# Chunked attention and two feed-forward layers: raw tiles of the next pair loaded from GpSimd's queue

## The chip, the cores and the metric

The kernel runs on one core of a Trainium2 chip. The metric is the device time of one execution in microseconds: 1698.02 us, the median of 3 runs (1697.63 to 1699.63). The core's engines run instruction streams of their own, each strictly in order: TensorE (PE; its weight loads are PEld), VectorE (DVE), ScalarE (ACT), GpSimd (POOL) and SyncE (SP). An engine waits for another through semaphores. A DMA is started by an instruction in the stream of one engine, called that engine's queue here, and is carried out by the core's 16 DMA engines; its completion raises a semaphore.

## The reference

```
attention, per batch (8), head (8) and chunk of 64 rows (576 = 9 chunks), head_dim 64:
    attn = softmax(q_c @ k_c^T / 8);   out_c = attn @ v_c
x = out as [4608 tokens, 512]
first layer:   h = x @ w_in;   g = s * relu(h)^2 + b;          y = g @ w_out     (512 -> 2048 -> 512)
second layer:  h = y @ w2_in;  g = h * sigmoid(1.702 * h);   out = g @ w2_out    (512 -> 2048 -> 512)
```

The weights of both layers come as float64 and are decoded to float32 on the chip. The change touches the second layer alone, and of it the way in which y is read back.

## The kernel before

The 4608 tokens are nine blocks of 512. Each float32 operand of a product is split into a high and a low part, and a product is three matmuls (low x high, high x high, high x low). The first layer runs block by block (L403 into h, L446 into acc) and stores its result y of each block to DRAM, features on partitions, as tiles y0 to y8 (y_140 to y_147 in listings are blocks 1 to 8). The second layer of block 0 runs the same way.

The other eight blocks of the second layer are computed in four pairs by `Halves`: features and tokens are both cut in two, and seven products M1 to M7 of sums of quarters stand for the eight products of the plain scheme. Each pair has two phases:

- First phase (L542): eight groups i of products, each of which leaves four quarters of h in PSUM banks named x, d and b. `keep` copies partial results out (L550, tile kept). `quarter` adds them (L561), takes the sigmoid (L563, tile r) and multiplies (L564) into g, held in tiles wo. Quarter "21" reads the bank x itself (L563 and L564 with the input x). Its bank is one of the tags acc0 to acc3; the last group, i = 7, has acc3.
- Second phase (L637): the seven products of g with the sums of w2_out. An operand is split by ACT (L614) and DVE (L615) into gh and gl, or op. M1's results need the banks acc2 and acc3, one for each half z of the output features.

The sums of the weights lie in DRAM (wi_sums, wo_sums) and are loaded by SP into tiles wi as these come free: L524 for the first phase, L597 for the second, 28 loads of 512 KB a pair. A tile wi comes free when PE has read it, so each of these loads waits for PE in SP's stream.

The operand x of the next pair is prepared while the present pair is in its second phase. `load_x(k)` (L481) loads four raw quarters of y into tiles xr of 128 x 512 float32 (256 KB each), for k = 0 and then for k = 1: b11, b12, b22 and b21, in that order. `operands_x(k)` then splits and subtracts them (L496 on ACT, L497 and L467 on DVE, tiles xh, xl and others). That is 8 loads a pair and 32 in all. The tiles xr come from the pool tpool (tag tmp, 10 buffers in rotation), which also holds kept, r and the output tiles ost; a load into one of them waits until the earlier user of that buffer has been read.

What sets the order: the program hands out its steps with due times (`plan`, `plan_first`, `plan_second`; the call `at`), sorted, and a scheduler then puts them into one fixed stream per engine. load_x(0) of the next pair falls due one unit after the second phase of the present pair begins, `operands_x(0)` three units later.

Of the kernel before, what the change touches and what calls it, by code (L numbers as in the profile page):

```python
# [59 lines left out]
def chunk_attention_two_ffn(ctx, tc, q, k, v, w1_in, w1_out, s, b, w2_in, w2_out, out):  # L60
# [6 lines left out]
    nc = tc.nc  # L67
# [37 lines left out]
    y_dram = [dpool.tile([P, KD, n], F32, name=f"y{j}") for j, n in enumerate(sizes)]  # L105
# [7 lines left out]
    def tmp(name, dtype=F32):  # L113
        return tpool.tile([P, NB_MAX], dtype, tag="tmp", name=name)
# [349 lines left out]
    HF, HK = KF // 2, KD // 2  # L464
# [4 lines left out]
    class Halves:  # L469
# [7 lines left out]
        def load_x(self, k):  # L477
            self.raw = getattr(self, "raw", {})
            for (a, c) in ((0, 0), (0, 1), (1, 1), (1, 0)):
                t = tmp("xr")  # L480
                nc.sync.dma_start(out=t, in_=y_dram[self.j + c][:, k + a * HK, :])  # L481
                self.raw[k, a, c] = t

        def x_place(self, n):
# [230 lines left out]
    for n, (i, kind) in enumerate((i, kind) for i in range(KF // 2) for kind in ("wi", "wo")):  # L715
        t = NS + 3 + 13.5 * n
# [45 lines left out]
```

## Time and profile before

| what | value |
|---|---|
| median of the runs | 1698.02 us |
| the profiled execution: time, and its span | 1698.26 us, 1696.5 us |
| mean granted TensorE clock | 0.984 |
| PE busy | 1603.6 us, 95% of the span |
| DVE / ACT / POOL busy | 1198.1 / 722.8 / 345.6 us |
| DMA moved | 263.79 MB, mean 155 GB/s |
| loads xr, all on SP | 32 of 256 KB, median 5.4 us from issue to landing |

How to read it: PE is the engine that is nearly always busy, so that time is lost where PE waits. The granted clock of 1.00 is TensorE's upper level, 2.4 GHz; its lower level is 1.2 GHz. POOL has no work after 973 us of the span. The four pairs run from about 1045 us to the end.

### The profile page before, as it was taken

To read this page: it belongs to the slowest core of one execution; us is meant where nothing else is said; L and a number is where in the kernel's file an instruction comes from. 1 tells how busy PE (TensorE), PEld (TensorE's weight loads), DVE (VectorE), ACT (ScalarE), POOL (GpSimd) and SP (SyncE) were. 2 spreads that over 40 slices of the span, in tenths; PEclk is the share of its full clock that TensorE was granted. 3 is DMA by queue.
4 is the path that set the end of the run, shared out by engine and by line. 5 is a ranking of instruction groups with operands and counts; after the bars stand their busy time and mean duration, and the time that the engine had idled before them with its cause. 6 is when DMAs were issued, how large, how long until landed. Compare 5 with 4: busy or idle time off the path is not lost.

```text
span 1696.5 us, 24510 instructions
## 1 busy us (share of the span) xinstructions
PE 1603.6 (95%) x8864; PEld 1317.1 (78%) x8864; DVE 1198.1 (71%) x1844; ACT 722.8 (43%) x1194; POOL 345.6 (20%) x310
## 2 busy tenths in 40 slices
PE   4767999999999999999999999989998999899998
PEld 3545788888878888888888888878886888688876
DVE  6999976868877686877833343579557946884685
ACT  3555533334333333433334433456345525553552
POOL 2677522222222223232315400000000000000000
PEclk9988999999999999999999999999999999999999
DMA  8733454655555465555324341667866686677664
GB/s 192 192 94 72 118 131 125 154 130 144 133 145 135 120 156 135 153 135 140 112 88 138 102 134 44 193 209 227 207 193 218 206 221 202 206 209 219 209 199 81
DMA packets 407128, 263.79 MB, mean 155 GB/s; under 512 B 264160, under 2 KB 354272, under 8 KB 407008
## 3 DMA queue, kind: packets, MB, share of 16 engines
q1 hardware_dynamic: 407008, 262.23, 56.4%
q8 instruction: 70, 1.15, 0.3%
q14 instruction: 50, 0.41, 0.1%
HBM read 205.52 MB, written 56.62 MB: 155 GB/s over the span
## 4 chain that ended last, share of the span: by engine, by line
PE 79%; DVE 12%; DMA 3%; SPq 2%; ACT 1%; issue 1%; POOL 0%; DVEq 0%; ACTq 0%; POOLq 0%
PE acc L446 21%; PE h L403 21%; PE x L637 10%; PE x L542 10%; PE d L637 5%; PE d L542 5%; PE b L637 3%; PE b L542 2%; DVE pt L300 2%; PE xT L308 2%; PE sc L274 1%; DVE r L412 1%; DMA xr<-y 1%; DMA wst<-in_moe_w_in 1%; SPq L246 1%
## 5 line engine op out<-in xcount | busy, mean ns | idle before, releaser
L403 PE MATMUL h<-xh,wi 128*128 128x512 f32 x1280 | 401.4, 395 | 9.5 <-ACT r L411 6.7
L446 PE MATMUL acc<-gh,wo 128*128 128x512 f32 x1152 | 359.2, 395 | 19.4 <-ACT gh L416 11.0
L403 PEld LDWEIGHTS h<-xh,wi 128*128 128x128 f32 x1280 | 242.3, 191 | 61.9 <-issue 10.0
L446 PEld LDWEIGHTS acc<-gh,wo 128*128 128x128 f32 x1152 | 216.8, 190 | 66.1 <-issue 9.4
L403 PE MATMUL h<-xl,wi 128*128 128x512 f32 x640 | 251.0, 393 | 0.0
L446 PE MATMUL acc<-gl,wo 128*128 128x512 f32 x576 | 224.4, 392 | 4.1 <-POOL gl L417 4.1
L412 DVE SCALAR_TENSOR_TENSOR r<-r,sb 128x512 f32<-128x512 f32 x144 | 137.2, 954 | 103.0 <-ACT r L411 102.5
L420 DVE SCALAR_TENSOR_TENSOR gl<-r,sb,gh 128x512 fp32r<-128x512 f32 x128 | 125.6, 981 | 70.6 <-ACT gh L419 70.4
L419 ACT ACTIVATE gh<-r,sb 128x512 fp32r<-128x512 f32 x128 | 92.6, 723 | 172.4 <-DVE r L412 171.6
L411 ACT ACTIVATE r<-h 128x512 f32<-128x512 f32 x144 | 85.1, 592 | 143.7 <-PE h L403 138.1
L403 PEld LDWEIGHTS h<-xl,wi 128*128 128x128 f32 x640 | 121.6, 190 | 25.8
L446 PEld LDWEIGHTS acc<-gl,wo 128*128 128x128 f32 x576 | 108.2, 188 | 27.9 <-POOL gl L417 4.9
L300 DVE STREAM_TRANSPOSE pt<-p 32x256 f32<-32x256 f32 x288 | 125.6, 436 | 4.8
L141 POOL TENSOR_TENSOR wm<-wm,wc 128x512 int32<-128x512 int32 x42 | 61.3, 1459 | 262.9 <-ACT gh L419 117.6
L614 ACT ACTIVATE op<-wo 128x512 fp32r<-128x512 f32 x128 | 79.9, 631 | 80.9 <-PE x L637 27.8
L564 DVE TENSOR_TENSOR wo<-wo,r 128x512 f32<-128x512 f32 x96 | 66.0, 691 | 63.4 <-ACT r L563 62.9
L637 PE MATMUL x<-op,wi 128*128 128x512 f32 x432 | 104.9, 390 | 0.0
L542 PE MATMUL x<-xh,wi 128*128 128x512 f32 x320 | 99.6, 391 | 3.3 <-DVE wo L561 3.1
L637 PEld LDWEIGHTS x<-op,wi 128*128 128x128 f32 x432 | 81.7, 189 | 17.3
L563 ACT ACTIVATE r<-wo 128x512 f32<-128x512 f32 x96 | 60.7, 633 | 76.5 <-DVE wo L561 75.8
L615 DVE TENSOR_TENSOR op<-wo,op 128x512 fp32r<-128x512 f32 x128 | 85.3, 680 | 7.4 <-ACT op L614 6.0
L467 DVE TENSOR_TENSOR wo<-wo 128x512 f32<-128x512 f32 x128 | 85.7, 684 | 0.8
(133 smaller groups left out, 2668.0 us busy)
## 6 DMA issues: line engine op xcount, KB each, us to landing
wi<-wo_sums SPq DMA_DIRECT2D x112, 512.0 KB, 4.3
wi<-wi_sums SPq DMA_DIRECT2D x96, 512.0 KB, 3.7
wi_sums<-wst SPq DMA_DIRECT2D x32, 448.0 KB, 3.6
wo_sums<-wst SPq DMA_DIRECT2D x32, 448.0 KB, 3.6
wst<-in_moe_w_in SPq DMA_DIRECT2D x21, 512.0 KB, 4.6
wst<-in_moe_w_out SPq DMA_DIRECT2D x21, 512.0 KB, 3.9
y<-ost SPq DMA_DIRECT2D x36, 256.0 KB, 3.1
wi<-wi_sums SPq DMA_DIRECT2D x32, 256.0 KB, 3.6
```

The lines of the kernel that those rows point to most:

```text
L300: nc.vector.transpose(out=pt[r.start + ek * BK:r.start + (ek + 1) * BK, :, eq * BK:(eq + 1) * BK], in_=p[r.start + eq * BK:r.start + (eq + ...
L403: nc.tensor.matmul(out=ps, lhsT=w_[:, kk, :], rhs=x_, start=kk == 0 and a == 0, stop=kk == KD - 1 and a == 2,)
L411: nc.scalar.activation(out=r, in_=ps, func=AF.Relu)
L412: nc.vector.scalar_tensor_tensor(out=r, in0=r, scalar=s_ap, in1=r, op0=ALU.mult, op1=ALU.mult)
L419: nc.scalar.activation(out=gh, in_=r, func=AF.Identity, bias=b_ap)
L420: nc.vector.scalar_tensor_tensor(out=gl, in0=r, scalar=b_ap, in1=gh.bitcast(F32), op0=ALU.add, op1=ALU.subtract)
L446: nc.tensor.matmul(out=acc[m], lhsT=l_, rhs=r_, start=i == 0 and a == 0, stop=i == KF - 1 and a == 2)
L467: nc.vector.tensor_tensor(out=to, in0=one, in1=two, op=ALU.subtract)
L542: nc.tensor.matmul(out=self.ps[key], lhsT=l_, rhs=r_, start=start and k == 0 and a == 0, stop=k == HK - 1 and a == 2, skip_group_check=not ...
L614: nc.scalar.activation(out=hi, in_=src, func=AF.Copy)
L615: nc.vector.tensor_tensor(out=lo, in0=src, in1=hi.bitcast(F32), op=ALU.subtract)
L637: nc.tensor.matmul(out=self.ps[key], lhsT=l_, rhs=r_, start=start and i == 0 and a == 0, stop=i == HF - 1 and a == 2, skip_group_check=not ...
```

## The change

One call in `load_x` names another engine. The 32 loads of xr are started by GpSimd instead of SyncE:

```diff
             for (a, c) in ((0, 0), (0, 1), (1, 1), (1, 0)):
                 t = tmp("xr")
-                nc.sync.dma_start(out=t, in_=y_dram[self.j + c][:, k + a * HK, :])
+                nc.gpsimd.dma_start(out=t, in_=y_dram[self.j + c][:, k + a * HK, :])
                 self.raw[k, a, c] = t
```

The streams of PE, DVE and ACT are the same in both kernels, instruction for instruction. SP's stream loses the 32 loads. At the place between the first and the second phase of the pair of blocks 1 and 2 (y_142 and y_143 are blocks 3 and 4, of the next pair), SP's stream reads, with - for before and + for now:

```order
 L524 DMA wi<-wi_sums_137 128x1024 x3
 L524 DMA wi<-wi_sums_137 128x512
-L597 DMA wi<-wo_sums 128x1024 x11
-L481 DMA xr<-y_142 128x512
-L481 DMA xr<-y_143 128x512 x2
-L481 DMA xr<-y_142 128x512
-L597 DMA wi<-wo_sums 128x1024 x9
-L481 DMA xr<-y_142 128x512
-L481 DMA xr<-y_143 128x512 x2
-L481 DMA xr<-y_142 128x512
-L597 DMA wi<-wo_sums 128x1024 x8
+L597 DMA wi<-wo_sums 128x1024 x28
```

The first four loads stood behind 11 loads of wo_sums and the next four behind 9 more; the 28 loads of wo_sums now follow one another. The same holds for the next two pairs. POOL's stream gains the loads at its end, behind its last work on the weights; its rows from there on are now:

```order
 L160 TENSOR_TENSOR wo<-wm,wo 128x512 x3
+L481 DMA xr<-y_140 128x512
+L481 DMA xr<-y_141 128x512 x2
+L481 DMA xr<-y_140 128x512 x2
+L481 DMA xr<-y_141 128x512 x2
+L481 DMA xr<-y_140 128x512
+L481 DMA xr<-y_142 128x512
+L481 DMA xr<-y_143 128x512 x2
+L481 DMA xr<-y_142 128x512 x2
+L481 DMA xr<-y_143 128x512 x2
+L481 DMA xr<-y_142 128x512
```

Nothing stands between the loads there, and the loads of the last two pairs follow in the same pattern. What a load waits for is, as before, its buffer of tpool and the earlier loads of its own queue. In the streams, the first load of a pair's four (b11) takes the buffer of the kept tile that quarter "22" of group 6 read, so it waits for that L561 on DVE; the second (b12) and the third (b22) wait for the two L564 after it, and the fourth (b21) for the L561 of quarter "11" of group 7.

## Rows read from the trace of the kernel before

**Rows 1.** Waits of PE from 1040 us on: engine, line, awaited: total us, times, longest.

```profile
PE x L637 <- DVE wo L564: 16.0, 4, 5.0
PE x L542 <- DVE wo L561: 3.1, 4, 0.8
```

**Rows 2.** Chain of waits, whole run: start us, us, what.

```profile
1129.13 6.32 DMA xr<-y
1139.47 8.11 PE x L637 x25
1148.94 5.44 PE d L637 x24
...
1290.60 7.00 DMA xr<-y
1300.32 7.92 PE x L637 x25
...
1451.12 6.20 DMA xr<-y
1461.34 7.55 PE x L637 x25
```

**Rows 3.** Chain of waits from 1600 to 1634 us, the last pair.

```profile
1616.70 0.61 ACT r L563
...
1618.07 5.97 PE x L637 x25
```

**Rows 4.** PE by time, at three places: start us, us, instruction [idle before <-releaser].

```profile
1133.96 0.84 PE L542 MATMUL x<-xo,wi 128*128 128x512 f32 x3
1139.47 1.22 PE L637 MATMUL x<-gh,wi 128*128 128x512 f32 x2 [4.67 <-DVE wo L564]
...
1300.32 1.22 PE L637 MATMUL x<-gh,wi 128*128 128x512 f32 x2 [4.99 <-DVE wo L564]
...
1461.34 1.12 PE L637 MATMUL x<-gh,wi 128*128 128x512 f32 x2 [4.88 <-DVE wo L564]
```

**Rows 5.** PE by time, the last pair.

```profile
1615.82 0.84 PE L542 MATMUL x<-xo,wi 128*128 128x512 f32 x3
1618.07 0.73 PE L637 MATMUL x<-gh,wi 128*128 128x512 f32 x2 [1.41 <-DVE wo L564]
```

**Rows 6.** Stretches: us, then busy us by engine, PEclk, DMA share, GB/s.

```profile
1139.47:1147.60 8.13, 8.13 (x26) 6.53 (x27) 8.10 (x14) 6.69 (x12) 0.00 (x0) 0.72 0.42 126
1618.10:1624.10 6.00, 6.00 (x26) 4.96 (x27) 4.59 (x8) 4.46 (x8) 0.00 (x0) 1.00 0.70 212
```

**Rows 7.** SP by time, first to second phase of the first pair.

```profile
1107.20 21.83 SPq L597 DMA_DIRECT2D wi<-wo_sums  x11
1129.13 1.86 SPq L481 DMA_DIRECT2D xr<-y  x4
```

**Rows 8.** Waits in SP's stream, 1107 to 1136 us.

```profile
SPq L597 <- PE x L542: 15.8, 8, 3.8
SPq L597 <- PE d L542: 7.0, 3, 2.3
```

**Rows 9.** ACT by time from 1128 us.

```profile
1128.86 1.22 ACT L563 ACTIVATE r<-wo 128x512 f32<-128x512 f32 x2 [1.42 <-DVE wo L561]
1135.48 0.63 ACT L496 ACTIVATE xh<-xr 128x512 fp32r<-128x512 f32 x1 [5.40 <-DMA xr<-y]
```

**Rows 10.** DVE by time from 1122 us.

```profile
1122.16 0.69 DVE L561 TENSOR_TENSOR wo<-x,kept 128x512 f32<-128x512 f32 x1 [0.22 <-PE x L542]
1123.37 1.29 DVE L564 TENSOR_TENSOR wo<-wo,r 128x512 f32<-128x512 f32 x2
1124.58 0.68 DVE L561 TENSOR_TENSOR wo<-b,kept 128x512 f32<-128x512 f32 x1
...
1127.47 0.69 DVE L564 TENSOR_TENSOR wo<-wo,r 128x512 f32<-128x512 f32 x1 [1.01 <-ACT r L563]
...
1136.75 0.68 DVE L467 TENSOR_TENSOR xr<-xr 128x512 f32<-128x512 f32 x1
1138.74 0.68 DVE L564 TENSOR_TENSOR wo<-x,r 128x512 f32<-128x512 f32 x1
...
1141.93 0.68 DVE L615 TENSOR_TENSOR gl<-wo,gh 128x512 fp32r<-128x512 f32 x1
```

**Rows 11.** DVE by time, the last pair.

```profile
1617.33 0.69 DVE L564 TENSOR_TENSOR wo<-x,r 128x512 f32<-128x512 f32 x1 [4.13 <-ACT r L563]
```

**Rows 12.** Loads of xr, whole run.

```profile
DMA to landing us min/median/max: 4.0/5.4/7.2
```

**Rows 13.** POOL's instructions grouped by line: count | busy us, mean ns.

```profile
L210 POOL TENSOR_TENSOR wst<-wst 128x896 fp32r<-128x896 f32 x32 | 68.3, 2134 | 34.1 <-ACT wst L209 34.1
L160 POOL TENSOR_TENSOR wi<-wm,wi 128x512 fp32r<-128x512 f32 x21 | 29.5, 1404 | 73.6 <-ACT wi L159 73.6
```

## The prediction

> **What bounds the kernel now.** I read the waits of PE first, since PE is busy 95% of the span and only its waits can be bought back. From 1040 us on, where the four pairs run, they come to little: 16.0 us in four waits of L637 for L564 on DVE, and 3.1 us in four waits for L561 [rows 1]. The reader is to see that the 16.0 us are three long waits of 4.67, 4.99 and 4.88 us [rows 4] and one of 1.41 us [rows 5], all at one place: where the second phase of a pair begins. M1's second output half needs the bank acc3, which quarter "21" of group 7 still has to read on ACT (L563) and DVE (L564).
>
> The chain of waits, read next, says why three are long: each has a load of xr in it, 6.32, 7.00 and 6.20 us from issue to use [rows 2]. The fourth pair prepares no next pair, has no such load, and its chain has only ACT's 0.61 us and DVE's 0.69 us there [rows 3, 11]. So the trace holds the same transition with and without the loads.
>
> By time, in the first pair: SP issues the four loads at 1129.13, behind 11 loads of wo_sums that took it 21.83 us [rows 7], because they wait for PE to free tiles wi (15.8 and 7.0 us of waits) [rows 8]. ACT has done with its earlier work at 1128.86 + 1.22 = 1130.08, and stands in L496 until 1135.48 for the first quarter b11 [rows 9]. Behind L496 in ACT's stream stands L563 of quarter "21", and behind L497 and L467 in DVE's stands its L564, which starts at 1138.74 [rows 10]; PE goes on at 1139.47. It had nothing to do from 1133.96 + 0.84 = 1134.80 [rows 4].
>
> A second cost follows. After the long wait the next 25 matmuls of L637 take 8.11, 7.92 and 7.55 us; in the last pair 5.97 us [rows 2, 3]. In that stretch the granted clock is 0.72, against 1.00 in the last pair's [rows 6]: part of it runs at the lower level of 1.2 GHz, after an idle of 4.67 us, and none after one of 1.41 us.
>
> **The change part by part.** It removes 32 loads from SP's stream and appends them to POOL's, which has no other work by then. What a load waits for on POOL is its buffer. For b11 that is the L561 of 1122.16 + 0.69 = 1122.85; for b12 and b22 the two L564 that run from 1123.37 to 1124.66, so about 1124.0 and 1124.7; for b21 the L561 that ends at 1124.58 + 0.68 = 1125.26 [rows 10]. So b11 can be issued 6.28 us before the 1129.13 of SP.
>
> When must it land? In the trace L564 of quarter "21" starts 1138.74 - 1135.48 = 3.26 us after L496 starts. In the last pair it starts 1617.33 - (1615.82 + 0.84) = 0.67 us after PE's last L542 [rows 5, 11]. For the first pair to do as well it must start at 1134.80 + 0.67 = 1135.47, so L496 at 1132.21 at the latest. From 1122.85 that is 9.36 us. b12 is first read by L467, 1136.75 - 1135.48 = 1.27 us after L496: by 1133.48, 9.4 us after its buffer is free. b22 and b21 are read only after L564. How long a load takes from POOL no row shows, as POOL issues no DMA here. From SP the 32 took 4.0 to 7.2 us, median 5.4 [rows 12], in bursts of four. I bound POOL's own part in a load below by 0 and above by 2.13 us, the dearest of its common instructions [rows 13], and take 1.4 us, its usual 128x512 step: 1.4 + 6.32 = 7.7 us for b11, and for b12, issued behind it, up to 1122.85 + 2 x 1.4 + 6.32 = 1131.97, both in time. At the upper bound b11 lands at 1122.85 + 2.13 + 7.2 = 1132.18, b12 at 1134.3, 0.8 us late. So nearly the whole gain is inside the bounds.
>
> The trace and a rule of the Trainium skill (DMA: Bandwidth & Descriptors, Issuing engines are not separate DMA queues) are to be weighed here. The rows show that the loads are late before any byte moves, by the waits in SP's stream. The rule says that DMAs of all issuing engines share the same 16 DMA engines and that spreading them saves only the sequencer's time to start them. Read strictly, it leaves nothing to gain and 1698.3 us; it is the third rival below. The same page (Specifications) gives about 1 us to the first byte for a load from GpSimd and 0.6 us from SyncE; my estimate from it is 0.4 us more a load, that is 6.7 us for b11 and the full gain.
>
> The sum, with the last pair as the model of a transition without the wait (idle and 25 matmuls: 1.41 + 5.97 = 7.38 us):
> - first: 4.67 + 8.11 - 7.38 = 5.40 us
> - second: 4.99 + 7.92 - 7.38 = 5.53 us
> - third: 4.88 + 7.55 - 7.38 = 5.05 us
>
> Together 15.98 us. Three costs I put at nothing. The x operands on ACT and DVE stay; of them L496, L497 and L467 before L564 move into the idle before 1134.80. DVE is busy for 8.10 of 8.13 us in the first pair's stretch after the wait, against 4.59 of 6.00 in the last pair's [rows 6], so I looked at whether DVE is late next: its first gl (L615) ends at 1141.93 + 0.68 = 1142.61, 3.2 us after L564's end at 1139.42. PE needs it after 21 matmuls, at the full rate of 5.44 / 24 = 0.227 us each [rows 2] 4.8 us after it goes on: 1.6 us to spare; without that cover each us is a us on PE, three times. SP's other loads lose only instructions in front of them, and they wait for PE. The four loads of 256 KB now run beside the last loads of wo_sums for products that start later; the DMA share was 0.42 in the stretch after the wait and 0.70 in the last pair's at full PE speed [rows 6], which leaves room. The chain waits for xr at the three transitions alone [rows 2], so the first eight loads, ahead of the first pair, bring nothing.
>
> The profiled execution is 1698.26 us (span 1696.5 and 1.76 around it), 0.24 above the median of the runs. 1698.26 - 15.98 = 1682.3 us.
>
> **The rivals.**
> 1. *POOL's issue is held by DVE.* DVE is busy almost without a break from 1122.16 on; if POOL's part needed DVE to pause, b11 would start in the gap before 1127.47 (1.01 us wide, from 1126.46) [rows 10] and land at 1126.46 + 7.0 = 1133.5, 1.3 us late; three times that is 4 us, so 1686 us. For: both work on the same memory. Against: POOL's common steps take about 1.4 us beside a busy DVE all through the run [rows 13]. The Trainium skill (SBUF — State Buffer, Who interferes with whom) has GpSimd's descriptor writing starved by DVE copies in their two-port modes; it excepts two-input tensor_tensor.
> 2. *POOL is slow to start a load, but not very.* With G us of POOL's time for each load in turn, b12 lands at 1122.85 + 2G + 6.32. The gain is whole up to G = 2.2 and gone at G = 3.8 (b12 at 1136.75, as now); in the middle 1690 us. For: no row shows a load from POOL. Against: L210, the dearest step, has 2.13 us for 896 columns of arithmetic [rows 13].
> 3. *No change.* The load is as late as before, since the DMA engines and not the issue decide, or its buffer comes free later than I read. 1698.3 us. Against: the 11 loads ahead wait for PE, not for the DMA engines [rows 8], and L561 of 1122.16 is 7 us ahead of the issue.
> 4. *Slower.* The same place with G above 3.8, from which it decides: at G = 5 b12 lands at 1139.2, 2.4 us later than it is read now, and b22 at 1144.2, where it holds back L615 and PE by up to 4.9 us. Three transitions: 7 to 15 us, 1705 to 1713 us. For: nothing excludes it, the four loads of a burst run in turn on one engine. Against: G = 5 is over twice POOL's dearest step.
>
> **How the numbers follow.** The forecast (1681.5 to 1683) has 0.70, rival 1 0.08, rival 2 0.08 (evenly from 1683 to 1697), rival 3 0.05, rival 4 0.09. What can be told from no change is 0.2%, 3.4 us. Faster: 0.70 + 0.08 + 0.08 = 0.86; same 0.05; slower 0.09. The range is 1680 to 1690: it holds the forecast with the scatter of the runs (2.0 us), rival 1 and half of rival 2, 0.82 in all. The lower end is 2.3 us below the forecast, for a wait after L542 somewhat shorter than the last pair's 1.41 us.
>
> **What would show it.** Right: in the waits of PE, L637 for L564 falls from 16.0 us to about 5.6 us (4 of 1.4), ACT no longer waits for xr at the transitions, the 25 matmuls after each take about 6.0 us at a granted clock of 1.00, and the loads on POOL start some 6 to 7 us ahead of ACT's L496. The chain has no xr in it. Wrong in a step: L496 still waits for xr (then the time from issue to landing says whether rival 1, 2 or 4), or the wait is gone and PE waits within the next 25 matmuls for L615 (DVE is late next), or it waits for wi (the loads of wo_sums lose against xr).

## The result, and the profile after

The changed kernel takes 1682.44 us (median of 5 runs, 1681.88 to 1683.44) against 1699.63 us (1697.63 to 1699.94) of the kernel before beside it: a ratio of 0.9904, 95% interval 0.9889 to 0.9918. That is 17.2 us between the medians, and by the interval 13.9 to 18.9 us. The forecast was 1682.3 us, 16.0 us less. In a second measurement the changed kernel took 1683.67 us against 1700.52 us, ratio 0.9900 (0.9885 to 0.9915).

The waits of PE from 1040 us on, in the kernel after (engine, line, awaited: total us, times, longest), answer to [rows 1]:

```profile
PE x L637 <- DVE wo L564: 5.8, 4, 1.5
PE x L542 <- DVE wo L561: 3.1, 4, 0.8
```

The 16.0 us have become 5.8 us, four waits of 1.4 to 1.5 us; the other row is as it was. PE by time at the start of each second phase answers to [rows 4] and [rows 5]:

```profile
1134.62 0.84 PE L542 MATMUL x<-xo,wi 128*128 128x512 f32 x3
1136.94 0.73 PE L637 MATMUL x<-gh,wi 128*128 128x512 f32 x2 [1.47 <-DVE wo L564]
...
1292.50 0.73 PE L637 MATMUL x<-gh,wi 128*128 128x512 f32 x2 [1.47 <-DVE wo L564]
...
1447.71 0.50 PE L637 MATMUL x<-gh,wi 128*128 128x512 f32 x1 [1.47 <-DVE wo L564]
...
1603.17 0.73 PE L637 MATMUL x<-gh,wi 128*128 128x512 f32 x2 [1.41 <-DVE wo L564]
```

The first three transitions now look like the fourth, which never had a load in it. The chain of waits around the first (start us, us, what) answers to [rows 2]; the load of xr has left it:

```profile
1129.35 4.76 PE x L637 x21
1134.11 1.37 PE x L542 x6
...
1135.56 0.61 ACT r L563
...
1136.19 0.70 DVE wo L564
...
1136.94 5.96 PE x L637 x25
```

The pieces left out are 0.02 to 0.04 us each. It reads: PE's last L542, then one activation, one multiplication, and PE again; the 25 matmuls take 5.96 us where they took 8.11. The stretch of these 25 matmuls (us, then busy us of PE, PEld, DVE, ACT and POOL, PEclk, DMA share, GB/s) answers to [rows 6]:

```profile
1136.94:1142.90 5.96, 5.96 (x26) 4.96 (x27) 5.92 (x10) 5.39 (x11) 1.62 (x3) 1.00 0.80 254
```

The granted clock is 1.00, the upper level, where it was 0.72. Next, DVE by time shows when the buffer of b11 comes free, POOL by time when the loads are issued, and ACT by time when they are used:

```profile
1122.82 0.69 DVE L561 TENSOR_TENSOR wo<-x,kept 128x512 f32<-128x512 f32 x1 [0.22 <-PE x L542]
```

```profile
1124.15 0.54 POOL L481 DMA_DIRECT2D xr<-y  x1 [125.92 <-ACT r L563]
1125.12 1.74 POOL L481 DMA_DIRECT2D xr<-y  x3 [0.43 <-DVE wo L564]
```

```profile
1130.11 0.63 ACT L563 ACTIVATE r<-wo 128x512 f32<-128x512 f32 x1 [0.22 <-DVE wo L561]
1130.65 0.61 ACT L496 ACTIVATE xh<-xr 128x512 fp32r<-128x512 f32 x1
1133.24 0.63 ACT L496 ACTIVATE xh<-xr 128x512 fp32r<-128x512 f32 x1 [1.98 <-DVE xr L467]
1135.56 0.60 ACT L563 ACTIVATE r<-x 128x512 f32<-128x512 f32 x1 [1.69 <-PE x L542]
```

The first POOL row names ACT's L563 as what ended POOL's idle time. That L563 ran from 1123.55 to 1124.18, past the issue at 1124.15, so b11 cannot have waited for it. b11 is issued 6.5 us before L496 reads it, and L496 starts with no wait, where [rows 9] show 5.40 us. L563 of quarter "21" waits for PE, as it should, and no longer behind a load.

### The profile page after: what moved, and what is told of

Its sections match the earlier page's. It is cut to its first block, busy times and chain, and to the rows that moved or that the text cites. A ratio compares the mean times of both kernels' runs of the same rounds, so it can differ in the third digit from the quotient of the medians.

```text
span 1681.6 us, 24541 instructions
## 1 busy us (share of the span) xinstructions
PE 1597.9 (95%) x8864; PEld 1312.7 (78%) x8864; DVE 1200.2 (71%) x1844; ACT 721.1 (43%) x1194; POOL 363.3 (22%) x342
## 4 chain that ended last, share of the span: by engine, by line
PE 81%; DVE 12%; DMA 2%; ACT 1%; issue 1%; SPq 1%; POOL 1%; DVEq 0%; POOLq 0%; ACTq 0%
PE acc L446 21%; PE h L403 21%; PE x L542 10%; PE x L637 10%; PE d L542 5%; PE d L637 5%; PE b L542 3%; PE b L637 3%; DVE pt L300 2%; PE xT L308 2%; DVE r L412 1%; PE sc L274 1%; DVE wo L144 1%; DVE gl L420 1%; DVE p L292 1%
## 5 line engine op out<-in xcount | busy, mean ns | idle before, releaser
L446 PE MATMUL acc<-gh,wo 128*128 128x512 f32 x1152 | 361.8, 397 | 20.0 <-ACT gh L416 11.6
L446 PEld LDWEIGHTS acc<-gh,wo 128*128 128x128 f32 x1152 | 218.6, 191 | 67.2 <-issue 9.4
L446 PE MATMUL acc<-gl,wo 128*128 128x512 f32 x576 | 225.3, 394 | 2.1 <-POOL gl L417 2.1
L446 PEld LDWEIGHTS acc<-gl,wo 128*128 128x128 f32 x576 | 108.9, 189 | 26.2 <-POOL gl L417 2.9
L481 POOL DMA_DIRECT2D xr<-y x32 | 17.4, 544 | 462.4 <-ACT r L563 262.4
L564 DVE TENSOR_TENSOR wo<-wo,r 128x512 f32<-128x512 f32 x96 | 66.0, 691 | 63.0 <-ACT r L563 62.6
L637 PE MATMUL x<-op,wi 128*128 128x512 f32 x432 | 104.4, 389 | 0.0
L542 PE MATMUL x<-xh,wi 128*128 128x512 f32 x320 | 99.7, 391 | 3.3 <-DVE wo L561 3.1
L637 PEld LDWEIGHTS x<-op,wi 128*128 128x128 f32 x432 | 81.1, 188 | 16.8
L563 ACT ACTIVATE r<-wo 128x512 f32<-128x512 f32 x96 | 60.7, 633 | 76.8 <-DVE wo L561 76.0
L615 DVE TENSOR_TENSOR op<-wo,op 128x512 fp32r<-128x512 f32 x128 | 85.3, 681 | 7.4 <-ACT op L614 6.0
```

Of the source, the lines that this page charges most:

```text
L446: nc.tensor.matmul(out=acc[m], lhsT=l_, rhs=r_, start=i == 0 and a == 0, stop=i == KF - 1 and a == 2)
L542: nc.tensor.matmul(out=self.ps[key], lhsT=l_, rhs=r_, start=start and k == 0 and a == 0, stop=k == HK - 1 and a == 2, skip_group_check=not ...
L564: nc.vector.tensor_tensor(out=g, in0=h, in1=r, op=ALU.mult)
L615: nc.vector.tensor_tensor(out=lo, in0=src, in1=hi.bitcast(F32), op=ALU.subtract)
L637: nc.tensor.matmul(out=self.ps[key], lhsT=l_, rhs=r_, start=start and i == 0 and a == 0, stop=i == HF - 1 and a == 2, skip_group_check=not ...
```

## The experiments

Two readings of the gain were set against each other. The queue theory is the prediction's: the loads were late only because they stood behind loads of wo_sums in one in-order stream, and any place that issues them in time does as well. The engine theory says that a load gains by being GpSimd's: another ring, another way of making descriptors, or relief of SP. Times are medians; the ratio to the kernel before, measured beside it, stands with its 95% interval.

### The queues swapped: wo_sums on GpSimd, xr on SP

```diff
 # load_wo, against the kernel before
-            nc.sync.dma_start(
+            nc.gpsimd.dma_start(
                 out=t, in_=wo_sums[:, p, 2 * r:2 * r + 2].rearrange("p f k a c -> p f (k a c)")
```

> Loads of xr stay on SP; the 112 loads of wo_sums move to GpSimd's queue instead. Queue theory (the xr loads were late only because they stood behind wo_sums loads in one stream): with nothing ahead of them on SP the xr loads are issued some 6 us earlier, PE's wait for L564 at each transition is about 1.4 us, 1682 us. Engine theory (a load gains by being GpSimd's, through another ring or descriptor path): xr on SP gains nothing, waits of 3.5 to 5 us stay, 1693 to 1699 us.

Measured: 1685.47 us, ratio 0.9920 (0.9905 to 0.9934). SP now issues the loads at 1124.23, and ACT's L496 does not wait for them:

```profile
1124.23 13.67 SPq L481 DMA_DIRECT2D xr<-y  x6
```

```profile
1131.32 0.61 ACT L496 ACTIVATE xh<-xr 128x512 fp32r<-128x512 f32 x1
```

PE's waits for L564 are those of the changed kernel, with xr on SP:

```profile
PE x L637 <- DVE wo L564: 5.8, 4, 1.5
PE x L542 <- DVE wo L561: 3.1, 4, 0.8
PE x L542 <- DMA wi<-wi_sums: 1.3, 2, 0.9
```

The transitions are as the queue theory has them, and the engine theory's 1693 to 1699 us did not come. The time is 3.5 us above the expected 1682; 1.3 us of it is a new wait for wi_sums, and the rest stays open. The scheduler also moved some 120 instructions of PE, DVE and ACT here, and some 160 in the next kernel; L496, L497 and L467 still stand ahead of L563 and L564 of quarter "21" in both.

### Both on GpSimd, in SP's old order

```diff
 # against the changed kernel: load_wo as in the swap above
-            nc.sync.dma_start(
+            nc.gpsimd.dma_start(
                 out=t, in_=wo_sums[:, p, 2 * r:2 * r + 2].rearrange("p f k a c -> p f (k a c)")
```

> Both the xr loads and the loads of wo_sums go through GpSimd's queue, 11 loads of wo_sums ahead of each first xr load as before on SP. Queue theory: the xr loads are issued as late as before and PE's wait comes back; the scheduler has put L564 of quarter 21 one step earlier behind L496 here (2.0 us behind it and not 3.3), so each wait is about 3.4 us and not 4.8: 1690 to 1695 us. Engine theory: xr is on GpSimd, so the gain stays: waits of 1.4 us, 1682 us.

Measured: 1699.13 us, ratio 0.9998 (0.9989 to 1.0007): no change from the kernel before, though every xr load is GpSimd's. POOL by time at the first transition:

```profile
1127.58 0.53 POOL L597 DMA_DIRECT2D wi<-wo_sums  x1 [2.22 <-PE d L542]
1128.94 0.53 POOL L597 DMA_DIRECT2D wi<-wo_sums  x1 [0.83 <-PE x L542]
1129.56 2.33 POOL L481 DMA_DIRECT2D xr<-y  x4
```

The last two of the 11 loads of wo_sums ahead wait for PE, and the xr loads are issued at 1129.56, 0.4 us later than SP did in [rows 7]. PE's waits for L564 are 14.3 us in four, the longest 4.4. I had expected 3.4 us each, and 1690 to 1695 us, which was missed: b11 was issued those 0.4 us later and took 6.8 us to its use (1129.56 to 1136.34) where it took 6.3 us before. With the swap this says which reading holds: xr does well on either engine when it is alone in its queue, and badly on either when it stands behind wo_sums.

### The loads from ScalarE's stream

```diff
-                nc.sync.dma_start(out=t, in_=y_dram[self.j + c][:, k + a * HK, :])
+                nc.scalar.dma_start(out=t, in_=y_dram[self.j + c][:, k + a * HK, :])
```

> The xr loads are issued from ScalarE's stream, where they stand behind the three L563 of group 7, just ahead of L496. Queue theory: a queue of its own is no help where the issue is late: b11 is issued at about 1130.1 on the clock of the kernel before, 1 us later than on SP, and lands 6.3 us later; waits of about 5.6 us, 1700 to 1702 us. Engine theory (another ring than SP's is what counts): waits shrink, 1682 to 1688 us.

Measured: 1699.71 us, ratio 1.0005 (0.9996 to 1.0015), just under the expected 1700 to 1702. ACT by time at the first transition (3 us later on the clock than in the kernel before, as PE is):

```profile
1132.75 0.63 ACT L563 ACTIVATE r<-wo 128x512 f32<-128x512 f32 x1 [0.22 <-DVE wo L561]
1132.76 1.78 ACTq L481 DMA_DIRECT2D xr<-y  x4
1139.13 0.63 ACT L496 ACTIVATE xh<-xr 128x512 fp32r<-128x512 f32 x1 [5.75 <-DMA xr<-y]
```

A queue of its own, with no load ahead, and no gain: the four loads stand behind three L563 and are issued where they are needed. PE's waits for L564 are 16.6 us; the 5.6 us each that I expected came out as at most 5.1.

### Fewer loads ahead on SP

```diff
 # against the kernel before: M6's loads of wo_sums fall due behind load_x(0) and are queued behind it
-                    at(base + 4 * n + r - 9, self.load_wo, n, r)
+                    at(base + 4 * n + r - 9 + (2.1 - 0.7 * r if n == 2 and r >= 0 else 0), self.load_wo, n, r)
 # load_x keeps its DMA as first_x[self.j, k]; load_wo:
+            x = first_x.get((self.j + 2, 0)) if n == 2 and r >= 0 else None
+            with tc.issue_after(x) if x else nullcontext():
```

This leaves 8 loads of wo_sums ahead of the first xr load in place of 11; with `r >= 2` in both places it leaves 10.

> Loads of xr on SP, but with 8 loads of wo_sums ahead of each first group in place of 11. Queue theory: the issue moves from 1129 to about 1124 (b21 to 1125, its buffer), so the loads are in time, PE's waits for L564 are 1.4 to 1.7 us: 1682 to 1685 us. Engine theory: xr is on SP as before, 1696 to 1699 us.

> The same with 10 loads of wo_sums ahead in place of 11. Queue theory with the deadline of the prediction: b11 is issued about 1.4 us earlier than before, at about 1127.8, and lands at about 1134.3, still past its deadline; L564 stands one step later behind L496 here (3.9 us): waits of about 4 us, of which a part costs the clock again, 1693 to 1698 us. If any head start were enough, 1685 us.

Measured: 1683.36 us, ratio 0.9902 (0.9887 to 0.9917), with 8 ahead; 1691.38 us, ratio 0.9956 (0.9941 to 0.9971), with 10. With 8 ahead SP issues xr at 1124.26 and PE waits 5.8 us in all for L568, which is this kernel's L564: the changed kernel's gain, with GpSimd left out of it. With 10 ahead, SP at the first transition, then PE at the other two (L643 is L637 here):

```profile
1129.80 1.80 SPq L484 DMA_DIRECT2D xr<-y  x4
```

```profile
1299.88 1.22 PE L643 MATMUL x<-gh,wi 128*128 128x512 f32 x2 [3.36 <-DVE wo L568]
...
1458.40 0.73 PE L643 MATMUL x<-gh,wi 128*128 128x512 f32 x2 [3.29 <-DVE wo L568]
```

PE comes to the first transition 2.0 us later in this kernel than in the kernel before, so the 1129.80 is a head start of 1.4 us. A part of the head start gives a part of the gain: waits of about 3.1 to 3.4 us against the 4 expected. The time was 2 us below the expected 1693. Against the kernel before the scheduler also moved some 100 instructions of PE, ACT and DVE. Between these two kernels it moved none of them: only six instructions of SP stand elsewhere, and the 8 us between the two times come of SP's order alone.

### Half of the loads

```diff
 # against the kernel before; the second run has k == 1
+                q = nc.gpsimd if k == 0 else nc.sync
-                nc.sync.dma_start(out=t, in_=y_dram[self.j + c][:, k + a * HK, :])
+                q.dma_start(out=t, in_=y_dram[self.j + c][:, k + a * HK, :])
```

> Only the loads of k=0 (the first four of each eight) go through GpSimd's queue, those of k=1 stay on SP. Queue theory: k=0 alone stands before quarter 21 of group 7, so the whole gain is here: 1682 to 1684 us, waits of 1.4 us. If the gain came from relieving SP's stream as such, about half: 1690 us.

> Only the loads of k=1 go through GpSimd's queue. Queue theory: nothing waits for PE's sake on these, no gain, 1697 to 1700 us, PE's waits as before at 4.7 to 5.0 us. If relieving SP's stream as such helped, about half the gain: 1690 us.

Measured: k = 0 alone 1683.44 us, ratio 0.9903 (0.9887 to 0.9920), the whole gain; k = 1 alone 1700.66 us, ratio 1.0002 (0.9991 to 1.0012), nothing. PE, DVE and ACT have the streams of the kernel before in both, so 16 loads out of the 32 carry all of it, and taking loads from SP is worth nothing in itself. In the second run the waits (L638 is L637, L565 is L564) came out somewhat longer than the 4.7 to 5.0 us expected, without a longer time; why stays open:

```profile
PE x L638 <- DVE wo L565: 17.5, 4, 5.9
```

### The operands of x behind quarter "21"

```diff
 # against the kernel before: quarter "21" of group 7 keeps its two instructions, L563 and L564
+            if (i, name) == (HF - 1, "21"):
+                behind[self.j + 2] = last
 # operands_x(0) of the next pair is queued behind them on ACT and DVE
+                    for ins in behind.get(self.j, ()) if k == 0 else ():
+                        es.enter_context(tc.issue_after(ins))
```

> Loads of xr on SP, as late as before; L496, L497 and L467 of the next pair's k=0 are put behind L563 and L564 of quarter 21 in the streams of ACT and DVE. If the late load costs PE time only because that quarter stands behind the operands of x in two in-order streams, PE's wait falls to 1.4 us although the loads land no earlier: 1681 to 1684 us. If PE's wait comes from the late load in another way (late operands, late gl), the waits stay at 4 to 5 us or return within the next 25 matmuls: 1692 to 1699 us.

Measured: 1685.07 us, ratio 0.9920 (0.9906 to 0.9935). SP and ACT by time at the first transition (L484 is L481, L575 is L563, L499 is L496 here):

```profile
1129.53 1.79 SPq L484 DMA_DIRECT2D xr<-y  x4
```

```profile
1129.24 1.23 ACT L575 ACTIVATE r<-wo 128x512 f32<-128x512 f32 x2 [1.42 <-DVE wo L573]
1135.29 0.60 ACT L575 ACTIVATE r<-x 128x512 f32<-128x512 f32 x1 [4.82 <-PE x L554]
1135.78 0.62 ACT L499 ACTIVATE xh<-xr 128x512 fp32r<-128x512 f32 x1
```

The loads are as late as in the kernel before, issued at 1129.53, and PE's waits for quarter "21" are 5.8 us in four all the same. So the late load cost PE time through the order of two instruction streams: L563 and L564, ready to run, stood behind L496, L497 and L467, which were not. The median is 1 us above what was expected; a new wait of PE for wi_sums, 1.5 us in two, is in it. The scheduler moved some 320 instructions of PE, DVE and ACT along with them, so the time alone would not show it; the ACT rows do, with L575 waiting for PE and L499 behind it.

### Other banks for the first phase

```diff
-                self.bank(key, BANK[m], f"acc{i % KD}")
+                self.bank(key, BANK[m], f"acc{(0, 1, 2, 3, 2, 3, 0, 1)[i]}")
```

> The changed kernel, and group i of the first phase takes the bank acc(0,1,2,3,2,3,0,1)[i] in place of acc(i mod 4), so that M1's two banks acc2 and acc3 were last used by groups 4 and 5 and not by 6 and 7. If the 1.4 us of PE's wait that is left at each of the four transitions is L563 and L564 of group 7 holding acc3, it goes: 5.7 us, 1676 to 1679 us. If another wait stands right behind it (the operand of group 7, or the earlier reuse of acc2 and acc3 by groups 4 and 5), no gain or a loss: 1682 to 1686 us.

> The same choice of banks with the loads of xr on SP, as late as before. The second output half of M1 can then run for 21 matmuls (4.8 us) before PE needs gl of group 7, which DVE gives about 3.2 us after L564 of quarter 21. If the bank acc3 is what ties PE to the late load, PE's waits fall from 4.7 to 5.0 us to about 3 us, behind L615 and not L564, three times, with less of the lower clock: 1688 to 1693 us. If the late load holds PE by another way, 1697 to 1700 us.

> The changed kernel once more, on the same chip as the two with other banks: 1682 to 1684 us by every theory.

Measured: 1690.66 us with xr on GpSimd, ratio 0.9941 (0.9929 to 0.9954); 1689.02 us with xr on SP, ratio 0.9928 (0.9915 to 0.9941); the changed kernel beside them 1683.67 us. The first is 7 us slower than the changed kernel and was expected 5.7 us faster: a miss, and what came is the second alternative of its expectation, another wait right behind, but dearer than the 1682 to 1686 us given for it. Its waits of PE, one of them by time, the L561 that it waits for, and the stretch after that:

```profile
PE x L542 <- DVE wo L561: 8.7, 4, 2.2
PE x L542 <- ACT kept L550: 0.8, 4, 0.2
```

```profile
1300.28 0.99 PE L542 MATMUL x<-xh,wi 128*128 128x512 f32 x2 [2.17 <-DVE wo L561]
```

```profile
1299.54 0.69 DVE L561 TENSOR_TENSOR wo<-x,kept 128x512 f32<-128x512 f32 x1
```

```profile
1300.00:1305.00 5.00, 4.72 (x14) 3.74 (x15) 5.00 (x10) 3.51 (x7) 0.54 (x1) 0.66 0.68 208
```

The waits for L564 are gone, but PE waits 2.2 us for L561 at each transition, and the mean granted clock of the stretch after it is 0.66. The product that this L561 reads ended at 1298.11; DVE came to it 1.4 us later, behind other work. In all PE waits 9.5 us here against the changed kernel's 8.9. The clock is 0.66 in such a stretch of 5 us at each of the four transitions; my estimate from that is 4 x 5 x 0.34 = 6.8 us, so it is the lower clock and not the waiting that costs nearly all of the 7 us. The second kernel has the same stream of PE and the same waits, though its loads are late; ACT at its third transition, where PE's last L542 ended at 1458.27:

```profile
1461.61 0.63 ACT L496 ACTIVATE xh<-xr 128x512 fp32r<-128x512 f32 x1 [4.10 <-DMA xr<-y]
1462.15 0.58 ACT L563 ACTIVATE r<-x 128x512 f32<-128x512 f32 x1
```

Quarter "21" starts 3.9 us after that product, behind the late load, and PE does not wait for it. So what ties PE to quarter "21" is indeed the bank: with it gone the late loads on SP cost nothing, and the two kernels differ by 1.6 us, within their intervals. I had expected the second kernel to wait about 3 us for L615; the scheduler made another order for PE, and no such wait is there. That 1689.02 us lies inside the expected 1688 to 1693 is luck, since another wait made the time.

### M4 of group 7 ahead of most of M1

```diff
 # against the changed kernel; self.last is PE's latest L542 (M4 of group 7 at this point)
+        def second_behind(self, n, i):
+            with tc.issue_after(self.last.ins):
+                self.second(n, i)
-                    at(t, self.second, n, i)
+                    at(t, self.second if n or i < 2 else self.second_behind, n, i)
```

> The changed kernel (xr on GpSimd), and M1's products of the second phase from i = 2 on are queued behind M4 of group 7 on PE, which stood behind 21 of them. The banks are as they were. L563 and L564 of quarter 21 then run beside 15 matmuls of M1's first half (3.4 us), and so acc3 is free when the second half comes. If the 1.47 us left at each of four transitions are only that order, PE's waits for L564 go from 5.8 us to under 1 us: 1676 to 1679 us. If M4 of group 7 is not ready so early (L561 of quarter 22) or gl of group 7 is late next, the wait moves to L542 or to L615: 1682 to 1686 us, or slower where the clock falls with it.

Measured: 1676.95 us (1676.30 to 1677.51), ratio to the kernel before 0.9869 (0.9852 to 0.9885): the fastest of all, 5 to 7 us below the changed kernel's two medians (1682.44 and 1683.67), which were not taken side by side with it. All its waits of PE from 1040 us on:

```profile
PE x L542 <- DVE wo L561: 3.1, 4, 0.8
PE x L542 <- DMA wi<-wi_sums: 1.2, 2, 0.7
```

PE has no wait for L564 left. The 1.4 to 1.5 us were the time of L563 and L564 after PE's last product of the first phase, and that product was last only by the scheduler's order. The operands of x stand behind quarter "21" on ACT and DVE here too, so this order should no longer need early loads. That is not shown: no run has this order with the loads on SP.

## Why the prediction was right

**The sum.** By its own terms (idle and 25 matmuls) the transitions now take 1.47 + 5.96 = 7.43 us, 1.47 + 5.96 = 7.43 and 1.47 + 5.97 = 7.44, against the 7.38 us taken from the last pair. The gains are 5.35, 5.48 and 4.99 us, 15.8 us in place of 15.98. The last pair was the right model because it is the same transition with the load left out. The profiled execution went from 1698.26 to 1683.40 us, 14.9 us; PE's last stretch of L446 ahead of the pairs begins 0.66 us later in it than in the one before (1045.27 against 1044.61), ahead of all three transitions. The profiles differ by 14.9 us and the medians by 17.2, so that the median of 1682.44 met the forecast within 0.2 us is luck; that the gain is near 16 us is not.

**When the loads start.** b11's buffer was free at 1122.82 + 0.69 = 1123.51 by DVE, and POOL issued it at 1124.15. I had counted no time between the two, and it was 0.64 us. Against SP's 1129.13 in [rows 7], moved by the 0.66 us, the head start is 5.6 us and not 6.28. The deadline had room for it.

**POOL's part in a load** was mis-sized: set at 1.4 us between bounds of 0 and 2.13, it measured 0.54 us a load (three in 1.74 us). DVE was busy beside it, and at this transition no load started more than the 0.64 us after its buffer was free, so rival 1 (DVE holds the issue) and rivals 2 and 4 (G above 2.2) fall on the same rows. The error could not be seen in the time, since at either size the loads were early enough.

**How long a load takes.** From issue to landing, first the 32 loads from GpSimd, then the same loads from SP in the swap:

```profile
DMA to landing us min/median/max: 3.1/5.7/7.9
```

```profile
DMA to landing us min/median/max: 3.4/5.8/8.9
```

In the kernel before it was 4.0 to 7.2, median 5.4, from SP [rows 12]. By the Trainium skill (DMA: Bandwidth & Descriptors, Specifications) the estimate was 0.4 us more a load from GpSimd. The medians of the two kernels differ by 0.3 us, but from SP alone they lie 0.4 us apart in two kernels, so these runs neither confirm nor refute the estimate.

**DVE late next.** After L564's end at 1136.19 + 0.69 = 1136.88 the first gl (L615) ended 3.2 us later, as counted, and PE did not wait for it, though DVE was busy for 5.92 of 5.96 us:

```profile
1139.39 0.69 DVE L615 TENSOR_TENSOR gl<-wo,gh 128x512 fp32r<-128x512 f32 x1
```

```profile
1143.64 0.62 PE L637 MATMUL x<-gl,wi 128*128 128x512 f32 x2
```

The prediction had counted 21 matmuls and 1.6 us to spare. PE reads gh for eight more matmuls first, in both kernels, and its next gl only at 1143.64: 3.6 us after this one was ready. The cover is wider than it was taken for.

**Rival 3**, that the DMA engines and not the issue decide, is excluded: the same bytes went through the same DMA engines in 1683 or 1691 us with 8 or 10 loads ahead, by SP's order alone, and in 1685 or 1699 us in the swap and its counterpart. The rule that stood beside it, in the Trainium skill (DMA: Bandwidth & Descriptors, Issuing engines are not separate DMA queues), has several issuing engines save only "the time on the sequencer it takes to initiate the DMA", and calls that usually small. Here the loads ahead in SP's stream waited for PE [rows 8], and 5 us a transition came of it; the measurement decides.

What rested on inference was that the lower clock after the long waits would go with them. The granted clock of 1.00 in all three stretches of the kernel after bears that out, and 8.11 - 5.96, 7.92 - 5.96 and 7.55 - 5.97 us make it 5.7 of the 15.8 us.

## What to carry to other kernels

Where a load is late, look first at what stands ahead of it in its issuing stream and what that waits for: a queue whose loads wait for buffers delays every load behind it, and another queue helps only if it is free at the right moment. Ask next why the late load costs anything; here two ready instructions stood behind one that was not, and reordering the streams of ACT and DVE gave nearly the same gain with the loads as late as before (ratio 0.9920 against 0.9904). And a stage of the same program that lacks the suspected cost is the best estimate of what its removal gives.

## What the runs showed of the hardware

A DMA instruction of 128 x 512 float32 took 0.54 us on GpSimd, and one of twice the bytes 0.53 us (112 loads of wo_sums, mean 529 ns); from SP, in the kernel before, the medians were 0.38 us and, for twice the bytes, 0.32 us. So the bytes did not set it.

The granted clock did not follow the length of the wait alone. In the kernel with 10 loads ahead PE idled 3.08, 3.36 and 3.29 us at three transitions, and the stretches of 25 matmuls after these were

```profile
1139.92:1148.75 8.83, 8.83 (x26) 7.04 (x27) 8.00 (x14) 6.44 (x12) 0.00 (x0) 0.65 0.41 125
1299.88:1307.33 7.45, 7.45 (x26) 6.05 (x27) 7.45 (x13) 6.18 (x12) 0.00 (x0) 0.78 0.42 108
1458.40:1464.36 5.96, 5.96 (x26) 4.96 (x27) 5.96 (x11) 5.86 (x12) 0.00 (x0) 1.00 0.50 140
```

at a mean of 0.65, 0.78 and 1.00 of the clock, so that the first two ran in part at the lower level. The same stretch cost 8.83, 7.45 or 5.96 us. With the other banks the clock fell after an idle of 2.17 us, and in the changed kernel it stayed at 1.00 after 1.47 us. What else decides it these runs do not show.
